# Last tile's columns in two pieces, the first FFN columns closed one by one, and another order for the first attention

## Chip, cores, metric

One core of a Trainium2 chip. The metric is the device time of one execution in microseconds (us), the median over several runs; lower is better. The profiler's span, from the first to the last recorded work of the core, is about 1.8 us shorter than the device time of the same run. Runs classed fast: for one core, executions up to 1.5% above the fastest.

## The reference, cut

```python
# q, k, v: (8 batches, 12 heads, 448, 64)
scores = q @ k.T / sqrt(64)
x = (maximum(scores, 0) ** 2 / 448) @ v          # -> (8, 448, 768)
xn = (x - mean) / sqrt(var + 1e-6) * g_ln
out = x + maximum(xn @ w_ch1, 0) @ w_ch2         # 768 -> 3072 -> 768
```

## The kernel before

The kernel carries its own list scheduler. Each piece of work is recorded with an estimated cost; TensorE's pieces are emitted in the program's order, and whatever the other engines can do by then is given to ScalarE or VectorE by estimated finish. What is built is fixed: each engine runs its list in order and waits on semaphores.

The attention of batch 0 has three groups of four heads (n = 0, 1, 2). For each, q and k are turned on TensorE ("T"), seven score blocks are made ("QK"), relu and square follow on ScalarE and VectorE, then seven products with v ("AV"). How the pieces interleave on TensorE is one string; `q` takes the next score piece, `a` the next of the others.

```python
FIRST_ORDER = "qaqqqqaqqqaaqqaaaaaqqaqqaqqaqaqqaaaaqqaaaqaaaaaaa"
...
av_stream = [("T", 0, 1)]        # turning of the far piece of k, columns 3 to 6 of group 0
for n in range(NPER):
    if n < NPER - 1:
        av_stream.append(("T", n + 1))
    av_stream += av_of(n)
    qk_stream += qks(n, 0, J)
...
for c in FIRST_ORDER:
    p = (av_stream if c == "a" else qk_stream).pop(0)
    PIECE[p[0]](*p[1:])
```

The rows of group 0 are loaded on SyncE's queue in three pieces (all of q; k columns 0 to 2; the "far" k columns 3 to 6); everything else is loaded on GpSimd's queue, at most eight transfers at a time. The score blocks 0 to 2 need the near piece of k only.

```python
for i, (t, j0, j1) in enumerate(((0, 0, J), FIRST[2], FIRST[3])):
    ...
    ld[t, j0] = R.add("SP", 480.0, emit, [], key=float(i), load=(2 * P, (46.0, 40.0, 90.0)[i]))
```

The first three columns of the first FFN product share 18 matmuls, and all three evictions wait for the last of them:

```python
for i, ki in enumerate(k_order(b)):
    def emit(eng, i=i, ki=ki):
        for ni in range(3):
            nc.tensor.matmul(st[ni][0], w1[:, ki, ni * P:(ni + 1) * P], xc[b][:, ki, :], ...)
    op = R.pe(570.0, emit, [ops["xc", b][i]] + ...)
for ni in range(3):
    h_evac(b, ni, st[ni], op, f_use if ni < 2 else slot_use)
```

The second FFN product makes each tile of 128 rows in two halves of 384 columns: 24 accumulating matmuls, one VectorE instruction that scales and adds x, then stores. The last tile (u = 3, m = 6) stores each half by itself.

Of the kernel before, what the change touches and what calls it, by code (L numbers as in the profile page):

```python
# [199 lines left out]
def kernel(  # L200
# [10 lines left out]
    nc = tc.nc  # L211
    P = 128
# [3 lines left out]
    Alu = mybir.AluOpType  # L216

    B, H, S, D = q.shape
    d_model = moe_g_ln.shape[0]
# [3 lines left out]
    K1 = d_model // P  # L223
# [4 lines left out]
    hd = d_model // 2  # L228
# [2 lines left out]
    POOL_BIAS = 1000.0  # L231
    N_FILL = 8

    FIRST_ORDER = "qaqqqqaqqqaaqqaaaaaqqaqqaqqaqaqqaaaaqqaaaqaaaaaaa"
    N_O = 2
    SUMMED = [0] + [2] + [NPER] * (B - 2)
    SQUARE_ON = (("DVE", "POOL"), (620.0, 1850.0))
# [19 lines left out]
    w1 = w_pool.tile([P, K1, d_ff], bf16)  # L257
    w2 = w_pool.tile([P, K2, d_model], bf16)
# [13 lines left out]
    def left(b):  # L272
        return slice(0, T) if b == 0 else slice(S - T, S)
# [12 lines left out]
    R = Order()  # L286
    stage, vt, qkT, xc, xm, mvs, rstd = {}, {}, {}, {}, {}, {}, {}
    ops = {}
# [8 lines left out]
    def big(tag, dims, **sizes):  # L297
        names = " ".join(sizes)
        n = 1
        for x in sizes.values():  # L300
            n *= x
        t = big_pool.tile([P, BIG], bf16, tag=tag)
        return t[:, :n].rearrange(f"p ({names}) -> p {names}", **sizes)
# [36 lines left out]
    def load_first():  # L340

        f = big_pool.tile([P, BIG // 2], fp32, tag=TURNED[1])
        raw = f[:, :4 * S].rearrange("p (t r c) -> p t r c", t=2, r=2)
        stage[0] = big(STAGE[0], None, t=2, r=H // 2, c=S)
        ld = {}
        for i, (t, j0, j1) in enumerate(((0, 0, J), FIRST[2], FIRST[3])):
            def emit(eng, t=t, cols=slice(j0 * D, j1 * D)):
                rows = (q, k)[t][0].rearrange("h (p j) d -> (h p) (j d)", j=J).rearrange("(pr r) c -> r pr c", r=P)
                nc.sync.dma_start(raw[:, t, :, cols], rows[:, 0::NPER, cols])  # L349
            ld[t, j0] = ld[t, j0 + 4] = R.add("SP", 480.0, emit, [], key=float(i), load=(2 * P, (46.0, 40.0, 90.0)[i]))  # L350
        ops["qk_ld", 0, 0] = []
        for t, j0, j1 in FIRST:
            cols = slice(j0 * D, j1 * D)

            def cast(eng, t=t, cols=cols):
                copy(eng, stage[0][:, t, 0::NPER, cols], raw[:, t, :, cols])
            ops["qk_ld", 0, 0].append(
                R.add(("DVE", "ACT"), (100.0 + 67.0 * (j1 - j0), 200.0 + 107.0 * (j1 - j0)), cast, [ld[t, j0]], key=-3.0))

    def copy(eng, o, i):  # L360
        if eng == "ACT":
            nc.scalar.copy(o, i)  # L362
        else:
            nc.vector.tensor_copy(o, i)  # L364
# [93 lines left out]
    def rows_of(t):  # L458
        return slice(t * T, (t + 1) * T)
# [414 lines left out]
    def k_order(b):  # L874
        return [pn + NPER * h for pn in range(NPER) for h in range(2)] if b < 2 else range(K1)

    def ffn_1_first(b):

        st = [{}, {}, {}]

        def fill(eng):
            for ni in range(2):
                ps = ps_f.tile([P, S], fp32, tag="f")
                st[ni][0] = ps
            ps = ps_s.tile([P, 2, 512], fp32, tag="s")
            st[2][0] = ps[:, 0, :S]
            for i in range(N_FILL):
                nc.tensor.matmul(st[i % 2][0][:, :3 * P], ones, x0_T[:, 0, S + T:], start=True, stop=True)
        R.pe(N_FILL * 163.0, fill, list(f_banks) + [slots[0]])
        for i, ki in enumerate(k_order(b)):  # L890
            def emit(eng, i=i, ki=ki):
                for ni in range(3):
                    nc.tensor.matmul(st[ni][0], w1[:, ki, ni * P:(ni + 1) * P], xc[b][:, ki, :],  # L893
                                     start=(i == 0), stop=(i == K1 - 1))
            op = R.pe(570.0, emit, [ops["xc", b][i]] + ([ops["w1", ni] for ni in range(3)] if i == 0 else []))
        for ni in range(3):
            h_evac(b, ni, st[ni], op, f_use if ni < 2 else slot_use)

    def ffn_1(b, ni):
# [18 lines left out]
    def h_evac(b, ni, st, op, use=f_use):  # L918
        def relu(eng):
            if b == 1:  # L920
                outs = ((h1[:, ni, 0:T], left(b)), (hb[ni // (K2 // 2)][:, ni % (K2 // 2), :], reg(b)))
            else:
                outs = ((h1[:, ni, h_cols(b)], slice(0, S)),)
            for o, c in outs:
                if eng == "ACT":
                    nc.scalar.activation(o, st[0][:, c], Act.Relu)  # L926
                else:
                    nc.vector.tensor_scalar(o, st[0][:, c], 0.0, None, op0=Alu.max)
        ev = R.add(("ACT", "DVE"), (560.0, 620.0) if b != 1 else (750.0, 740.0), relu, [op], key=-3.0)
        use(ev)  # L930
        ops["h", b, ni] = ev
        if ni == K2 - 1:
            ops["f1_end", b] = op

    o_st = {}
    o_ring = [DONE] * N_O

    def f2_deps(u, m, j, part, parts):
        n = K2 // parts
        b = 2 * u + (0 if m < 3 else 1)  # L940
        d = [ops["w2", (part + 1) * n - 1], ops["h", b, (part + 1) * n - 1]]
        if part == 0:
            d.append(f_banks[0])
        return d

    def ffn_2(u, m, j, part, parts):
        def stat(ki):
            if u == 0:
                if m <= 3:
                    c = m + 1 if m < 3 else 0  # L950
                    return h1[:, ki, c * P:(c + 1) * P]
                return hb[ki // (K2 // 2)][:, ki % (K2 // 2), (m - 4) * P:(m - 3) * P]
            if m < 3:
                return h1[:, ki, T + m * P:T + (m + 1) * P]
            if m == 3:
                return h1[:, ki, 3 * P:4 * P]
            return h1[:, ki, (m - 4) * P:(m - 3) * P]

        b = 2 * u + (0 if m < 3 else 1)

        def emit(eng):
            if part == 0:
                o_ps = ps_f.tile([P, hd], fp32, tag="f")
                o_st["ps"] = o_ps
            n = K2 // parts
            for ki in range(part * n, (part + 1) * n):
                nc.tensor.matmul(o_st["ps"], stat(ki), w2[:, ki, j * hd:(j + 1) * hd],  # L967
                                 start=(ki == 0), stop=(ki == K2 - 1))
        op = R.pe(975.0 * 4 / parts, emit, f2_deps(u, m, j, part, parts))
        if (m in (2, 6) or (u, m) == (0, 3)) and j == 1 and part == parts - 1:  # L970
            ops["f2_end", b] = op
        if part < parts - 1:
            return
        ps = o_st["ps"]
        ri = m if m < 3 else m - 3

        def evac(eng):
            if j == 0:
                o_t = o_pool.tile([P, d_model], fp32, tag="o")
                o_st[u, m] = o_t  # L980
            nc.vector.scalar_tensor_tensor(  # L981
                o_st[u, m][:, j * hd:(j + 1) * hd], ps, rstd[b][:, ri:ri + 1],
                xm[u, m][:, j * hd:(j + 1) * hd], op0=Alu.mult, op1=Alu.add)
        ev = R.add("DVE", 620.0, evac, [op, ops["rstd", b], o_ring[-N_O]], key=-3.0)
        f_use(ev)
        if j == 1:
            if m in (2, 6) or (u, m) == (0, 3):
                ops["f2_out", b] = ev
            if m == 3:
                ops["m3_out", u] = ev  # L990
        final = (u, m) == (B // 2 - 1, 6)
        if j == 0 and not final:
            return
        cols = slice(j * hd, (j + 1) * hd) if final else slice(0, d_model)
        blocks = {0: ((0, 0), (0, 1)), 1: ((0, 2), (0, 3)), 2: ((0, 4), (0, 5)), 3: ((1, 6), (0, 6)),
                  4: ((1, 0), (1, 1)), 5: ((1, 2), (1, 3)), 6: ((1, 4), (1, 5))}[m]
        if u == 0 and m <= 3:
            blocks = {0: ((0, 1), (0, 2)), 1: ((0, 3), (0, 4)), 2: ((0, 5), (0, 6)), 3: ((1, 6), (0, 0))}[m]
        for r, (bb, jj) in enumerate(blocks):
            def store(eng, r=r, bb=bb, jj=jj):  # L1000
                dst = out[2 * u + bb].rearrange("(p j) d -> j p d", j=J)[jj, :, cols]
                (nc.scalar if eng == "ACT" else nc.sync).dma_start(dst, o_st[u, m][rows_of(r), cols])
            sto = R.add("SP" if final and r else "ACT", 550.0, store, [ev], key=-0.5, load=(T, 150.0))
        o_ring.append(sto)
# [162 lines left out]
    with tc.manual_schedule():  # L1167
# [31 lines left out]
        means = 0  # L1199
        for c in FIRST_ORDER:  # L1200
            p = (av_stream if c == "a" else qk_stream).pop(0)
# [20 lines left out]
        for b in range(2, B):  # L1222
            u = b // 2
# [41 lines left out]
```

## Time and profile before

| | before |
|---|---|
| three runs | 541.95, 542.58, 542.9 us, median 542.58 |
| with three more beside the changed kernel | median 542.27 |
| the profiled run | 543.12 us, span 541.3 us |
| TensorE busy | 528.2 us, 98% of the span |
| first FFN group begins, after which TensorE has no listed idle | 30.03 us |

The rows behind this table are shown in the prediction. In a row of the view in order of time, the first number is the start in us, the second the time to the end of the group, then engine, source line, operation, destination and source, shape and count; the bracket is the engine's idle time before it and what ended it.

### The profile page before, as it was taken

What the parts mean: (1) busy time and instruction counts of PE and PEld (TensorE: products, weight loads), DVE (VectorE), ACT (ScalarE), POOL (GpSimd) and SP (SyncE); (2) the same over time, 40 slices, a digit from 0 to 9 for tenths busy, and PEclk for the clock granted to TensorE, in tenths of its full rate; (3) what the DMA queues carried; (4) which work ended last, traced back from release to release, by engine and by line L of the source; (5) the groups of instructions that cost most, each with busy time, mean ns of one, the idle gap of its engine ahead of it and who ended that gap; (6) DMA issues with size and microseconds to landing.
All of it is one profiled execution on the core that took longest, in us unless ns stands there. A gap on an engine that the chain in (4) does not pass through costs nothing.

```text
span 541.3 us, 9868 instructions
## 1 busy us (share of the span) xinstructions
PE 528.2 (98%) x4200; PEld 285.7 (53%) x4200; DVE 281.9 (52%) x483; ACT 232.6 (43%) x381; POOL 112.5 (21%) x129
## 2 busy tenths in 40 slices
PE   4899999999999999999999999999999999999996
PEld 3444455555554455555555455555555555555564
DVE  5988647438674556835366446752456525530011
ACT  5977612115425652556124653265422654044200
POOL 6411600221260124311061121600220102100000
PEclk9999999999999999999999999999999999999999
DMA  9999999997299204970189602990023100510022
GB/s 194 194 187 192 200 183 170 149 147 133 60 155 142 62 1 91 195 117 1 31 106 188 94 1 47 165 192 1 1 58 76 29 1 1 99 49 1 1 58 59
DMA packets 141400, 51.83 MB, mean 96 GB/s; under 512 B 121254, under 2 KB 137132, under 8 KB 141356
## 3 DMA queue, kind: packets, MB, share of 16 engines
q0 software_dynamic: 81072, 25.50, 43.5%
q1 hardware_dynamic: 55804, 14.88, 18.6%
q10 hardware_dynamic: 4480, 10.82, 7.2%
q8 instruction: 33, 0.54, 0.4%
q14 instruction: 11, 0.09, 0.0%
HBM read 51.91 MB, written 11.01 MB: 116 GB/s over the span
## 4 chain that ended last, share of the span: by engine, by line
PE 95%; DVE 3%; DMA 1%; issue 0%; SPq 0%; ACT 0%; DVEq 0%
PE o_ps L967 41%; PE ps L910 40%; PE sc L569 7%; PE ps L631 6%; DVE a L593 1%; DMA f<-in_k_dram 1%; PE ps L893 1%; DVE a L580 1%; PE ps L490 0%; DVE t L364 0%; PE ps L697 0%; PE slot L806 0%; SPq L349 0%; ACT a L834 0%; DVE a L845 0%
## 5 line engine op out<-in xcount | busy, mean ns | idle before, releaser
L910 PE MATMUL ps<-a,w 128*128 128x448 bf16 x1134 | 220.5, 353 | 0.0
L967 PE MATMUL o_ps<-w,h 128*128 128x384 bf16 x1200 | 199.9, 326 | 0.0
L910 PEld LDWEIGHTS <-w 128*128 128x128 bf16 x1134 | 108.3, 98 | 108.3 <-issue 10.6
L967 PEld LDWEIGHTS <-h 128*128 128x128 bf16 x1200 | 116.0, 98 | 81.6 <-issue 5.8
L926 ACT ACTIVATE h<-ps 128x448 bf16<-128x448 f32 (+1 forms) x168 | 89.2, 532 | 103.8 <-PE ps L910 102.0
L578 ACT ACTIVATE a<-sc 128x896 bf16<-128x896 f32 x102 | 90.3, 924 | 86.5 <-PE sc L569 84.2
L580 DVE TENSOR_SCALAR a<-sc 128x896 bf16<-128x896 f32 x57 | 62.0, 1087 | 108.9 <-PE sc L569 108.7
L593 DVE TENSOR_TENSOR a<-a 128x896 bf16<-128x896 bf16 x158 | 99.2, 669 | 2.4 <-ACT a L578 2.1
L981 DVE SCALAR_TENSOR_TENSOR o_t<-o_ps,r_t,x_all 128x384 f32<-128x384 f32 x56 | 34.4, 615 | 107.1 <-PE o_ps L967 106.8
L726 POOL TENSOR_TENSOR sum_t<-sum_t,xT_all 128x384 f32<-128x384 f32 (+2 forms) x25 | 19.4, 778 | 167.4 <-ACT xT_all L362 154.4
L569 PE MATMUL sc<-t 64*64 64x448 bf16 x672 | 48.6, 368 | 2.2 <-ACT a L578 1.2
L631 PE MATMUL ps<-a,v_t 64*64 64x448 bf16 x636 | 36.8, 353 | 0.7 <-DVE t L364 0.5
L724 POOL TENSOR_TENSOR sum_t<-xT_all 128x384 f32<-128x384 bf16 (+2 forms) x13 | 10.2, 791 | 124.7 <-DVE a L593 96.5
L834 ACT ACTIVATE a<-a,g_sb 128x448 bf16<-128x448 bf16 x38 | 22.2, 656 | 25.9 <-DVE a L827 24.8
L362 ACT CAST xT_all<-ps 128x768 bf16<-128x768 f32 (+3 forms) x39 | 22.2, 573 | 22.6 <-PE ps L631 14.6
L569 PEld LDWEIGHTS <-t 64*64 64x64 bf16 x672 | 17.5, 107 | 25.6 <-issue 18.5
L631 PEld LDWEIGHTS <-v_t 64*64 64x64 bf16 x672 | 20.0, 107 | 14.7 <-issue 3.9
L400 POOL DMA_DIRECT2D t<-in_q_dram x12 | 19.3, 1772 | 24.3 <-DMA t<-t 22.9
L967 PE MATMUL o_ps<-w,t 128*128 128x384 bf16 x144 | 23.7, 326 | 0.0
L400 POOL DMA_DIRECT2D t<-in_k_dram x12 | 23.7, 2526 | 0.0
L827 DVE TENSOR_TENSOR a<-xT_all,sum_t 128x768 bf16<-128x768 bf16 (+1 forms) x24 | 19.4, 852 | 6.7 <-ACT sum_t L819 6.5
L384 POOL DMA_DIRECT2D v_t<-in_v_dram x16 | 16.5, 1402 | 19.5 <-DMA w<-in_moe_w_ch_dram 11.1
(55 smaller groups left out, 183.4 us busy)
## 6 DMA issues: line engine op xcount, KB each, us to landing
out_dram<-o_t ACTq DMA_DIRECT2D x54, 192.0 KB, 2.8
v_t<-in_v_dram POOLq DMA_DIRECT2D x16, 336.0 KB, 15.0
w<-in_moe_w_ch_dram POOLq DMA_DIRECT2D x4, 1152.0 KB, 40.1
t<-in_q_dram POOLq DMA_DIRECT2D x12, 336.0 KB, 7.2
t<-in_k_dram POOLq DMA_DIRECT2D x12, 336.0 KB, 10.8
w<-in_moe_w_ch_dram POOLq DMA_DIRECT2D x4, 768.0 KB, 19.6
w<-in_moe_w_ch_dram POOLq DMA_DIRECT2D x1, 1536.0 KB, 29.5
t<-in_q_dram POOLq DMA_DIRECT2D x5, 224.0 KB, 10.1
```

What stands on the lines that cost most here:

```text
L362: nc.scalar.copy(o, i)
L400: nc.gpsimd.dma_start(stage[b][half * T:(half + 1) * T, t].rearrange("p j (h d) -> p j h d", d=D), src[b, half * 6:half * 6 + 6].rearrange ...
L569: nc.tensor.matmul(sc[rows_of(half), r, :S], qkT[b][rows_of(r), 1, s * NPER + pn, rows_of(half)], qT[:, :, pn, rows_of(half)], start=True, ...
L578: nc.scalar.activation(attn[n, s], st[0][:, :, :S], Act.Relu, scale=rc2)
L580: nc.vector.tensor_scalar(attn[n, s], st[0][:, :, :S], rc2, 0.0, op0=Alu.mult, op1=Alu.max)
L593: nc.vector.tensor_mul(attn[n, s], attn[n, s], attn[n, s])
L631: nc.tensor.matmul(av_st[n][half][rows_of(hh)], vt[b][rows_of(half), 2 * pn + hh, s * D:(s + 1) * D], attn[n, s][rows_of(half), hh, :], st ...
L834: nc.scalar.mul(o, o, g_sb[:, ki:ki + 1])
L910: nc.tensor.matmul(st[0], w1[:, ki, ni * P:(ni + 1) * P], xc[b][:, ki, :], start=(i == 0), stop=(i == K1 - 1))
L926: nc.scalar.activation(o, st[0][:, c], Act.Relu)
L967: nc.tensor.matmul(o_st["ps"], stat(ki), w2[:, ki, j * hd:(j + 1) * hd], start=(ki == 0), stop=(ki == K2 - 1))
L981: nc.vector.scalar_tensor_tensor(o_st[u, m][:, j * hd:(j + 1) * hd], ps, rstd[b][:, ri:ri + 1], xm[u, m][:, j * hd:(j + 1) * hd], op0=Alu. ...
```

## The change

Its intent: the last eviction and store get smaller (128 columns in place of 384); the first FFN columns can be evicted earlier; the first attention's order is made for a k piece that lands later than was assumed (the load's figure goes from 90 to 120, which is an estimate that the scheduler uses and no instruction).

```diff
--- before.py
+++ after.py
@@ -231,7 +231,7 @@
     POOL_BIAS = 1000.0
     N_FILL = 8
 
-    FIRST_ORDER = "qaqqqqaqqqaaqqaaaaaqqaqqaqqaqaqqaaaaqqaaaqaaaaaaa"
+    FIRST_ORDER = "qqaqaqqqqqqaaaqaqaaqaqaqqqaaaqaaqaaqqaaqqaaaaaaaa"
     N_O = 2
     SUMMED = [0] + [2] + [NPER] * (B - 2)
     SQUARE_ON = (("DVE", "POOL"), (620.0, 1850.0))
@@ -347,7 +347,7 @@
             def emit(eng, t=t, cols=slice(j0 * D, j1 * D)):
                 rows = (q, k)[t][0].rearrange("h (p j) d -> (h p) (j d)", j=J).rearrange("(pr r) c -> r pr c", r=P)
                 nc.sync.dma_start(raw[:, t, :, cols], rows[:, 0::NPER, cols])
-            ld[t, j0] = ld[t, j0 + 4] = R.add("SP", 480.0, emit, [], key=float(i), load=(2 * P, (46.0, 40.0, 90.0)[i]))
+            ld[t, j0] = ld[t, j0 + 4] = R.add("SP", 480.0, emit, [], key=float(i), load=(2 * P, (46.0, 40.0, 120.0)[i]))
         ops["qk_ld", 0, 0] = []
         for t, j0, j1 in FIRST:
             cols = slice(j0 * D, j1 * D)
@@ -887,13 +887,19 @@
             for i in range(N_FILL):
                 nc.tensor.matmul(st[i % 2][0][:, :3 * P], ones, x0_T[:, 0, S + T:], start=True, stop=True)
         R.pe(N_FILL * 163.0, fill, list(f_banks) + [slots[0]])
-        for i, ki in enumerate(k_order(b)):
-            def emit(eng, i=i, ki=ki):
-                for ni in range(3):
-                    nc.tensor.matmul(st[ni][0], w1[:, ki, ni * P:(ni + 1) * P], xc[b][:, ki, :],
-                                     start=(i == 0), stop=(i == K1 - 1))
-            op = R.pe(570.0, emit, [ops["xc", b][i]] + ([ops["w1", ni] for ni in range(3)] if i == 0 else []))
+        k = k_order(b)
+
+        def part(cols, i0, i1):
+            def emit(eng):
+                for i in range(i0, i1):
+                    for ni in cols:
+                        nc.tensor.matmul(st[ni][0], w1[:, k[i], ni * P:(ni + 1) * P], xc[b][:, k[i], :],
+                                         start=(i == 0), stop=(i == K1 - 1))
+            return R.pe(190.0 * len(cols) * (i1 - i0), emit, ops["xc", b][i0:i1] + [ops["w1", ni] for ni in cols])
+        for i in range(K1 - 2):
+            part(range(3), i, i + 1)
         for ni in range(3):
+            op = part([ni], K1 - 2, K1)
             h_evac(b, ni, st[ni], op, f_use if ni < 2 else slot_use)
 
     def ffn_1(b, ni):
@@ -943,7 +949,13 @@
             d.append(f_banks[0])
         return d
 
-    def ffn_2(u, m, j, part, parts):
+    def ffn_2(u, m, j, part, parts, c0=0, c1=hd):
+        final = (u, m) == (B // 2 - 1, 6)
+        if final and j == 1 and c1 - c0 == hd:
+            if part == 0:
+                ffn_2(u, m, j, 0, 1, 0, 2 * P)
+                ffn_2(u, m, j, 0, 1, 2 * P, hd)
+            return
         def stat(ki):
             if u == 0:
                 if m <= 3:
@@ -964,9 +976,9 @@
                 o_st["ps"] = o_ps
             n = K2 // parts
             for ki in range(part * n, (part + 1) * n):
-                nc.tensor.matmul(o_st["ps"], stat(ki), w2[:, ki, j * hd:(j + 1) * hd],
+                nc.tensor.matmul(o_st["ps"][:, :c1 - c0], stat(ki), w2[:, ki, j * hd + c0:j * hd + c1],
                                  start=(ki == 0), stop=(ki == K2 - 1))
-        op = R.pe(975.0 * 4 / parts, emit, f2_deps(u, m, j, part, parts))
+        op = R.pe(975.0 * 4 / parts * (c1 - c0) / hd, emit, f2_deps(u, m, j, part, parts))
         if (m in (2, 6) or (u, m) == (0, 3)) and j == 1 and part == parts - 1:
             ops["f2_end", b] = op
         if part < parts - 1:
@@ -979,19 +991,18 @@
                 o_t = o_pool.tile([P, d_model], fp32, tag="o")
                 o_st[u, m] = o_t
             nc.vector.scalar_tensor_tensor(
-                o_st[u, m][:, j * hd:(j + 1) * hd], ps, rstd[b][:, ri:ri + 1],
-                xm[u, m][:, j * hd:(j + 1) * hd], op0=Alu.mult, op1=Alu.add)
-        ev = R.add("DVE", 620.0, evac, [op, ops["rstd", b], o_ring[-N_O]], key=-3.0)
+                o_st[u, m][:, j * hd + c0:j * hd + c1], ps[:, :c1 - c0], rstd[b][:, ri:ri + 1],
+                xm[u, m][:, j * hd + c0:j * hd + c1], op0=Alu.mult, op1=Alu.add)
+        ev = R.add("DVE", 160.0 + 1.2 * (c1 - c0), evac, [op, ops["rstd", b], o_ring[-N_O]], key=-3.0)
         f_use(ev)
         if j == 1:
             if m in (2, 6) or (u, m) == (0, 3):
                 ops["f2_out", b] = ev
             if m == 3:
                 ops["m3_out", u] = ev
-        final = (u, m) == (B // 2 - 1, 6)
         if j == 0 and not final:
             return
-        cols = slice(j * hd, (j + 1) * hd) if final else slice(0, d_model)
+        cols = slice(j * hd + c0, j * hd + c1) if final else slice(0, d_model)
         blocks = {0: ((0, 0), (0, 1)), 1: ((0, 2), (0, 3)), 2: ((0, 4), (0, 5)), 3: ((1, 6), (0, 6)),
                   4: ((1, 0), (1, 1)), 5: ((1, 2), (1, 3)), 6: ((1, 4), (1, 5))}[m]
         if u == 0 and m <= 3:
```

## The prediction

> **What bounds the kernel now.** I read the page first, then the chain that ended last, then the first 30 us of each engine in order of time, then the last 20 us. The page's engine totals and slices (one digit is a fortieth, 13.5 us; tenths of the slice):
>
> ```profile
> span 541.3 us, 9868 instructions
> PE 528.2 (98%) x4200; PEld 285.7 (53%) x4200; DVE 281.9 (52%) x483; ACT 232.6 (43%) x381; POOL 112.5 (21%) x129
> ...
> PE   4899999999999999999999999999999999999996
> ...
> PEclk9999999999999999999999999999999999999999
> ```
>
> TensorE (PE) is full from the third slice to the last but one, at full clock. PE's own time order lists no idle after this row:
>
> ```profile
> 30.03 3.56 PE L893 MATMUL ps<-a,w 128*128 128x448 bf16 x18 [0.18 <-ACT a L834]
> ```
>
> So the time is three terms: the 30.03 us before PE becomes continuous, PE's work from there, and the tail after the last matmul. PE work can only be moved between places in the middle. The chain of waits at the end:
>
> ```profile
> 506.06 31.21 PE o_ps L967 x192
> 537.27 0.03 issue
> 537.30 0.62 DVE o_t L981
> ```
>
> Each 384-column matmul costs 31.21 us / 192 = 162.6 ns; the last eviction ends at 537.92, and 541.3 - 537.92 = 3.4 us go to issuing and landing the last store. The first 30 us are otherwise: PE waits many times, and VectorE (DVE) and ScalarE (ACT) run nearly without gaps from 9 us on. The rows that matter, in order of time:
>
> ```profile
> 6.78 0.59 PE L569 MATMUL sc<-t 64*64 64x448 bf16 x4 [0.73 <-DVE t L364]
> 7.42 0.92 ACT L578 ACTIVATE a<-sc 128x896 bf16<-128x896 f32 x1 [2.65 <-PE sc L569]
> 7.69 0.43 DVE L364 CAST t<-f 128x512 bf16<-128x512 f32 x1 [0.97 <-DMA f<-in_k_dram]
> 8.18 0.53 PE L490 MATMUL ps<-identity,t 64*64 64x64 bf16 x12 [0.81 <-DVE t L364]
> 8.52 0.83 POOL L424 DMA_DIRECT2D w<-in_moe_w_ch_dram  x1 [1.23 <-DMA t<-in_q_dram]
> 8.86 0.42 DVE L364 COPY t<-ps 128x512 bf16<-128x512 bf16 x1 [0.73 <-PE ps L490]
> ...
> 9.24 2.54 ACT L578 ACTIVATE a<-sc 128x896 bf16<-128x896 f32 x3 [0.91 <-PE sc L569]
> ...
> 10.17 0.70 POOL L332 DMA_DIRECT2D t<-in_q_dram  x1 [0.82 <-DMA t<-in_k_dram]
> ...
> 18.80 4.36 DVE L593 TENSOR_TENSOR a<-a 128x896 bf16<-128x896 bf16 x8
> ```
>
> What to see: the first scores come at 6.78. PE then stands 0.81 us for the far piece of k (landed about 7.67), whose turning comes next in its fixed order; ACT waits 0.91 us for the second scores. The two POOL rows date two loads: POOL's ninth load is held until the first is in (q of the second third of the heads, 8.52), the tenth until the second (k of it, 10.17).
>
> **What the Trainium skill says.** "TensorE: Matmul & The Clock Gate", section "Back-to-back issue gap": N/2.4 + 2.5 ns per matmul when warm, but for a stream of weight load plus matmul about 81 ns at N=128 and 131 at N=512. The trace has 162.6 ns at N=384, exactly the formula (160 + 2.5), and nothing like 131 at 512; N=128 with a full weight load occurs nowhere in it. The section "LDWEIGHTS (loading the stationary operand)" of that page gives P/1.2, or 107 ns for 128 columns; the trace has 98 ns. Whether that is the spacing at N=128 or only a latency the trace can't tell: 64-column loads show 107 to 124 ns each though 51 transposes, each with its own load, pass in 1.60 us. "DMA: Bandwidth & Descriptors", section "Latency and other measured facts", puts the fixed cost of a transfer at about 2 us; the trace agrees, the last 96 KB stores land 2.3 to 2.4 us after issue. So a smaller last store saves little.
>
> **The change, part by part.**
>
> (1) Last tile, second half. Before: 24 matmuls of 384 columns, one eviction, one pair of stores. After: 24 of 256, 24 of 128 with all 24 weight loads repeated (the built order has 24 matmuls and 24 loads more), two evictions, two pairs of stores. By the formula that the trace bears out, the 256 piece is 24 x 109.2 = 2.62 us. The 128 piece is 24 x 55.8 = 1.34 us if matmuls bind, 24 x 81 = 1.94 by the skill's stream figure, 24 x 98 = 2.35 if weight loads run one after another at their recorded length. I choose about 65 ns, nearer to the formula, since the formula was right at 384: 1.56 us. Sum 4.18 against 24 x 162.6 = 3.90: +0.28. The last eviction shrinks: evictions of the FFN's first product take 548 ns at 384 columns and 224 at 64, a slope of 1.01 ns per column; 615 - 256 x 1.01 = 356 ns, saving 0.26. The last store has rows of 512 B for 1,536 B; of the 2.3 us to landing I give it 0.15. The built waits show that the last eviction waits for PE alone, not for the stores of the piece before, and those were issued earlier: the 256 piece is evicted some 0.48 us after its 2.62 (0.486 for 256 columns), its issue (about 0.45) ends before the 128 piece is evicted. Tail: +0.28 - 0.26 - 0.15 = -0.13 us.
>
> (2) First three columns of the FFN closed one by one. The same 18 matmuls, no new instruction: four steps of three, then the last two steps column by column. Column 0 closes four matmuls (4 x 0.19 = 0.75 us) earlier and column 1 two. But PE went straight on with score matmuls at 33.59 and had no idle there, so nothing waits that could be given back. A cost may lie in the sixth centred piece being wanted at matmul 14 instead of 16: 30.03 + 13 x 0.19 = 32.5, and DVE's two gains end at 32.42. Just in time. Effect 0 to +0.05.
>
> (3) Order of the first attention. Same pieces, 27 of one kind and 22 of the other. After: two score blocks before the far k piece is turned (one before), then one more, then turning the second third at once, then six score blocks; before it did three score blocks first. Consequences, chased by hand with the durations above (first matmul of a score block to its relu 0.64 us, relu 0.83 in a row on ACT, 1.00 on DVE, squares 4.36/8, so 0.54):
> the second scores run at 7.15 and their relu follows the first at 8.25, not at 9.24: ACT gains 0.9. But DVE's order still puts the copy of the far piece (8.86, because k lands at 7.67) ahead of the first square, so DVE starts no earlier. The third relu ends near 10.0. Now PE stands at the k half of the second turning until 10.17, turns until about 11.0, and only then makes the fourth scores: relu at 11.6. ACT is idle 1.6 us where before it was idle 0.9. DVE's work from 8.86 to the last square: before 20 squares, 3 relus, 4 turned copies, 2 output copies = 10.8 + 3.0 + 2.0 + 1.1 = 16.9; after 20, 2, 5, 3 = 10.8 + 2.0 + 2.6 + 1.6 = 17.0. ACT gets a relu more (19 for 18) and loses a turned copy and an output copy. Chasing both on, the last square ends on DVE near 26.2 and on ACT near 26.4, against 26.3 and 26.1 before. Effect about +0.05 on the 30.03, with an error of my chase of some 0.5 either way. The larger load figure (120 for 90) is no instruction; it only shifts what the kernel's own scheduler believes.
>
> Further on the built order of PE shows only regroupings of FFN pieces with attention, of equal work: 0.
>
> Sum: -0.13 + 0.02 + 0.05 = -0.06; I lean a little towards gain, because a tuned order was presumably picked for one: 542.58 - 0.2 = 542.4 us.
>
> **Rivals.** (a) Weight loads bind at 128 columns: 2.35 us in place of 1.56, the tail grows by 0.66, about 543.2. For: 98 ns recorded. Against: the overlapping small loads. (b) PE's new early wait for the k load is longer or starves ACT and DVE both: start +0.5, 542.9 to 543.1. For: the load at 10.17 stands just ahead of six score blocks. Against: DVE has 17 us of work in any order and two squares and a copy to fill with. (c) The order pays: DVE loses its small holes, ACT finishes early since it has less to do, start -0.7, and the tail -0.35 at 56 ns: 541.5. For: ACT's sum shrinks by about 0.6. Against: DVE's does not. (d) The earlier closing frees banks and PE gains: nothing for it, as PE has no idle there.
>
> **Range and chances.** The three runs before spread 541.95 to 542.9, about 0.5 each way; start and tail add about 0.5 each. Range 541.4 to 543.3. Two per cent is 10.9 us, more than all idle in the start; nothing in reach does that: faster 0.01, same 0.98, slower 0.01.
>
> **What would show it.** In the changed profile: PE's continuous stretch begins at 29.5 to 30.5 (start); the L569 row after the second turning begins near 11.0 with ACT idle before its relu about 1.6 (my chase); the first FFN group shows no idle inside; the 24 last matmuls take 1.3 to 1.9 us; the last eviction 0.36 us, and 3.2 to 3.3 us from its end to the span's. I would be wrong if PE becomes continuous more than 1 us earlier or later, if the 128 piece takes over 2.2 us, or if a new idle appears in the middle.

## Result, and the profile after

| | before | after |
|---|---|---|
| median, six runs each | 542.27 us | 541.71 us |
| range | 541.95 to 542.9 | 541.68 to 542.41 |
| ratio of fast runs | | 0.9991, 95% interval 0.9978 to 1.0004 |
| span of the profiled run | 541.3 us | 539.9 us |
| first FFN group begins | 30.03 us | 28.93 us |
| last eviction begins | 537.30 us | 536.39 us |
| from there to the end of the span | 4.0 us | 3.5 us |

A ratio is the mean time of the one kernel's fast runs over that of the other's in the same rounds, so it isn't quite the ratio of the medians. The interval includes 1: this is "same" by the 2% rule, and even the 0.1% is not clear of noise as a plain comparison.

The page of the changed kernel, its span and engine totals (busy us, share, instructions):

```profile
span 539.9 us, 9924 instructions
PE 526.8 (98%) x4224; PEld 287.0 (53%) x4224; DVE 282.6 (52%) x487; ACT 231.3 (43%) x378; POOL 112.6 (21%) x129
```

There are 24 matmuls and weight loads more, as built. The changed kernel's VectorE in order of time at the end (the last two rows are the two pieces), and its chain of waits at the end (start, us, what):

```profile
532.43 0.62 DVE L993 SCALAR_TENSOR_TENSOR o_t<-o_ps,r_t,x_all 128x384 f32<-128x384 f32 x1 [3.28 <-PE o_ps L979]
...
535.05 0.48 DVE L993 SCALAR_TENSOR_TENSOR o_t<-o_ps,r_t,x_all 128x256 f32<-128x256 f32 x1 [2.00 <-PE o_ps L979]
...
536.39 0.35 DVE L993 SCALAR_TENSOR_TENSOR o_t<-o_ps,r_t,x_all 128x128 f32<-128x128 f32 x1 [0.85 <-PE o_ps L979]
```

```profile
505.10 31.27 PE o_ps L979 x216
...
536.39 0.35 DVE o_t L993
```

Evictions start as soon as their matmuls are done, so the distances between their starts are the matmul times: 535.05 - 532.43 = 2.62 us for 24 matmuls of 256 columns (109.2 ns each), and 536.39 - 535.05 = 1.34 us for 24 of 128 columns (55.8 ns each), against 3.90 us for the undivided half. Splitting costs 0.06 us of TensorE. The last eviction fell from 0.62 to 0.35 us, and from its end to the end of the span it is 539.9 - 536.74 = 3.16 us against 3.38.

The start of the changed kernel, in order of time, from TensorE, ScalarE, VectorE and GpSimd:

```profile
6.80 0.96 PE L569 MATMUL sc<-t 64*64 64x448 bf16 x8 [0.74 <-DVE t L364]
7.55 0.53 PE L490 MATMUL ps<-identity,t 64*64 64x64 bf16 x11
...
28.93 3.56 PE L896 MATMUL ps<-a,w 128*128 128x448 bf16 x18 [0.18 <-ACT a L834]
```

```profile
7.44 2.54 ACT L578 ACTIVATE a<-sc 128x896 bf16<-128x896 f32 x3 [2.62 <-PE sc L569]
10.22 8.30 ACT L578 ACTIVATE a<-sc 128x896 bf16<-128x896 f32 x10 [0.24 <-PE sc L569]
```

```profile
6.66 0.42 DVE L364 CAST t<-f 128x512 bf16<-128x512 f32 x1
8.22 0.42 DVE L364 COPY t<-ps 128x512 bf16<-128x512 bf16 x1 [1.15 <-PE ps L490]
```

```profile
7.23 0.88 POOL L424 DMA_DIRECT2D w<-in_moe_w_ch_dram  x1
8.05 0.76 POOL L332 DMA_DIRECT2D t<-in_q_dram  x1
```

The far piece of k is cast at 6.66 us, without a wait, where the profile of the kernel before has it at 7.69 after a wait for the load. The transfers' own view gives the landing of this piece (the last number is us from issue to landing), before and after:

```profile
f<-in_k_dram SPq DMA_DIRECT2D x1, 256.0 KB, 5.9
```

```profile
f<-in_k_dram SPq DMA_DIRECT2D x1, 256.0 KB, 3.9
```

The issue begins at 1.77 us in both, so the piece landed at about 7.7 and at about 5.7. The six further kernels below that load nothing more have 3.9 to 4.9 and the cast at 6.65 to 6.74: VectorE came to the cast only then, so in these profiles a landing up to about 6.7 us delays nothing. The two GpSimd rows had waited until 8.52 and 10.17 for earlier loads; here they don't wait at all. None of these loads depends on anything that was changed. So the two profiles differ by 1.10 us at the FFN group for two reasons mixed together, the order and when the loads landed, and the pair alone can't tell them apart.

### The profile page after: what moved, and what is told of

The parts are those of the page before. It is cut to its first block, busy times and chain, and to the rows that moved or that the text cites. A ratio compares the mean times of both kernels' runs of the same rounds, so it can differ in the third digit from the quotient of the medians.

```text
span 539.9 us, 9924 instructions
## 1 busy us (share of the span) xinstructions
PE 526.8 (98%) x4224; PEld 287.0 (53%) x4224; DVE 282.6 (52%) x487; ACT 231.3 (43%) x378; POOL 112.6 (21%) x129
## 4 chain that ended last, share of the span: by engine, by line
PE 95%; DVE 2%; ACT 1%; DMA 1%; issue 0%; ACTq 0%; DVEq 0%
PE o_ps L979 41%; PE ps L916 40%; PE sc L569 6%; PE ps L631 5%; DVE a L593 1%; PE ps L490 1%; DVE t L364 1%; PE ps L896 1%; DMA f<-in_q_dram 1%; ACT a L578 1%; PE ps L697 0%; PE slot L806 0%; DVE xT_all L364 0%; DVE a L580 0%; ACT a L834 0%
## 5 line engine op out<-in xcount | busy, mean ns | idle before, releaser
L979 PE MATMUL o_ps<-w,h 128*128 128x384 bf16 (+2 forms) x1224 | 200.1, 323 | 0.0
L979 PEld LDWEIGHTS <-h 128*128 128x128 bf16 x1224 | 117.4, 98 | 80.4 <-issue 5.7
L993 DVE SCALAR_TENSOR_TENSOR o_t<-o_ps,r_t,x_all 128x384 f32<-128x384 f32 (+2 forms) x57 | 34.7, 608 | 104.8 <-PE o_ps L979 104.6
L384 POOL DMA_DIRECT2D v_t<-in_v_dram x16 | 16.5, 1401 | 20.9 <-DMA w<-in_moe_w_ch_dram 18.0
## 6 DMA issues: line engine op xcount, KB each, us to landing
w<-in_moe_w_ch_dram POOLq DMA_DIRECT2D x1, 1536.0 KB, 29.2
```

The source lines that it names most:

```text
L979: nc.tensor.matmul(o_st["ps"][:, :c1 - c0], stat(ki), w2[:, ki, j * hd + c0:j * hd + c1], start=(ki == 0), stop=(ki == K2 - 1))
L993: nc.vector.scalar_tensor_tensor(o_st[u, m][:, j * hd + c0:j * hd + c1], ps[:, :c1 - c0], rstd[b][:, ri:ri + 1], xm[u, m][:, j * hd + c0:j ...
```

## Experiments

Two theories stood at this point. *Order*: the new order brings the FFN group from about 30 to about 28.9. *Loads*: the 1.1 us is mostly a difference in landing between two executions, which any kernel would show. Twelve kernels ran; the kernel before ran on the same chip. All gave correct results. All twelve are classed "same" at 2%, so what follows rests on profiles and on comparing groups of runs.

### The order alone

```diff
-    FIRST_ORDER = "qaqqqqaqqqaaqqaaaaaqqaqqaqqaqaqqaaaaqqaaaqaaaaaaa"
+    FIRST_ORDER = "qqaqaqqqqqqaaaqaqaaqaqaqqqaaaqaaqaaqqaaqqaaaaaaaa"
-  load=(2 * P, (46.0, 40.0, 90.0)[i])
+  load=(2 * P, (46.0, 40.0, 120.0)[i])
```

> The kernel before with only the new order of the first attention and the larger load figure. Theory 'order': continuous work on the first FFN matmul group begins about 28.9 us, where the changed kernel's profile has it, whatever the loads do, and the time falls by 0.3 to 1.1 us. Theory 'loads': the 1.1 us between the two profiles is mostly a difference in when the early loads landed in those two executions; then the time falls by under 0.2 us when runs with equally early loads are compared, the runs of both kernels spread over about 0.7 us in two groups, and in the profile the start of the FFN group follows the landing of the far k piece: near 28.9 with that cast at 6.7, near 30 with it at 7.7. The tail from the last matmul's end to the span's end stays as before, about 4.0 us.

Measured: 542.12 us median (542.08 to 542.20, and one run of 543.03), the kernel before beside it 542.07 (541.79 to 543.4); ratio 1.0 (0.9988 to 1.0013). The cast of the far piece was at 6.74 and the FFN group began at 28.98. From the last eviction's start to the span's end 4.05 us, as before. The order alone shows no gain: its four lower runs average 0.17 us more than the lower group of the kernel before, which the next experiment defines.

### The split tail alone

```diff
+        if final and j == 1 and c1 - c0 == hd:
+            if part == 0:
+                ffn_2(u, m, j, 0, 1, 0, 2 * P)
+                ffn_2(u, m, j, 0, 1, 2 * P, hd)
+            return
```

(with the column bounds of the change; old order, old closing.)

> The kernel before with only the last tile's second half in 256 and 128 columns. From the two profiles: the two pieces take 2.62 and 1.34 us where the one took 3.90 (+0.06), the tail from last matmul to end falls from 4.03 to 3.53 (-0.50). If these stand apart from the rest: time lower by 0.3 to 0.45 us than the kernel before, that is most of the whole change's 0.56 between medians. If the order is what pays: lower by no more than 0.2.

Measured: 541.86 us median of six: 541.29, 541.54, 541.83, 541.88, then 543.08 and 543.36. The first four average 541.63; of the 35 runs of the kernel before, the 21 below 542.4 (a cut made after the runs were seen) average 541.96. So 0.33 less, as expected, for runs of the lower group. In the profile (541.29 us) the last eviction begins 507.33 us after the FFN group (before 507.27, so +0.06), and the span ends 3.5 us later (before 4.0). And here is the old order with early loads, which no profile had shown yet (VectorE, then TensorE, in order of time):

```profile
6.66 0.42 DVE L364 CAST t<-f 128x512 bf16<-128x512 f32 x1
7.85 0.42 DVE L364 COPY t<-ps 128x512 bf16<-128x512 bf16 x1 [0.77 <-PE ps L490]
```

```profile
28.70 3.56 PE L893 MATMUL ps<-a,w 128*128 128x448 bf16 x18 [0.18 <-ACT a L834]
```

The old order begins the FFN group at 28.70, *earlier* than the new order's 28.93. So the 30.03 of the first profile was a run with late loads, and theory "order" has fallen.

### The closing alone

```diff
+        for i in range(K1 - 2):
+            part(range(3), i, i + 1)
         for ni in range(3):
+            op = part([ni], K1 - 2, K1)
             h_evac(b, ni, st[ni], op, f_use if ni < 2 else slot_use)
```

> The kernel before with only the first three FFN columns closed one by one. Both theories: no change (under 0.1 us), as TensorE has no idle after that group in either profile; the first of the three evictions starts 1.2 to 1.4 us after ScalarE's last gain in place of 1.6. A rival would be that earlier free banks let TensorE gain: 0.3 us or more.

Measured: 542.14 us median (lower group of four 542.01 to 542.22, two at 543.43 and 543.88); ratio 1.0005 (0.9992 to 1.0019). In the profile the 18 matmuls take 3.56 us as before, and the first eviction starts 1.22 us after ScalarE's last gain, where before it was 1.60. TensorE and ScalarE in order of time:

```profile
28.75 3.56 PE L896 MATMUL ps<-a,w 128*128 128x448 bf16 x18 [0.18 <-ACT a L834]
...
31.59 0.54 ACT L932 ACTIVATE h<-ps 128x448 bf16<-128x448 f32 x1 [1.22 <-PE ps L896]
```

TensorE doesn't notice: the first matmul of the second FFN product begins 67.20 us after the FFN group in both kernels. Later a difference appears: the matmul that sums for the fourth batch's mean begins 185.30 us after the group, before 185.16, and the same 0.13 us stays to the last eviction (507.40 against 507.27). In between the scheduler, whose estimates had moved, grouped second-product matmuls and attention pieces otherwise; the number of changes between tiled and full matmuls is the same in both. Why that grouping takes 0.13 us more was not settled. It goes with the grouping and not with the closing as such: the kernel of "One exchange in the order" below has the closing and the split tail, its matmul for the fourth batch's mean begins 185.16 us after the group, and its last eviction 507.32, which is 507.27 and the tail's 0.06.

### The changed kernel with the old order

```diff
-    FIRST_ORDER = "qqaqaqqqqqqaaaqaqaaqaqaqqqaaaqaaqaaqqaaqqaaaaaaaa"
+    FIRST_ORDER = "qaqqqqaqqqaaqqaaaaaqqaqqaqqaqaqqaaaaqqaaaqaaaaaaa"
```

(and 90 for 120.)

> The changed kernel with the old order and load figure put back. Theory 'loads' (order worth nothing): the same time as the changed kernel within 0.15 us in runs with equally early loads, 0.3 to 0.45 below the kernel before. Theory 'order': 0.3 us or more above the changed kernel, and the FFN group begins about 30 us.

Measured: 542.33 us median, in two groups: 541.5, 541.54, 541.73 and 542.93, 543.16, 543.25. The lower group is 0.12 us below the changed kernel's five (541.71). Its profile has early loads too. TensorE in order of time, the turning of the far piece and the FFN group:

```profile
7.16 0.52 PE L490 MATMUL ps<-identity,t 64*64 64x64 bf16 x11
...
28.69 3.56 PE L896 MATMUL ps<-a,w 128*128 128x448 bf16 x18 [0.18 <-ACT a L834]
```

(VectorE's copy of the turned piece begins at 7.84, against 7.85 in the profile of the tail alone.) This explains the 0.24 us. In the old order the far piece is turned at 7.16, right behind the first score block; in the new one a second score block runs first and the turning begins at 7.55. From the copy of the turned piece (7.84 old, 8.22 new), VectorE runs almost without gaps to the last square, so a later copy is a later everything. It also shows that what follows the copy is a little *shorter* in the new order: 28.93 - 8.22 = 20.71 against 28.69 - 7.84 = 20.85.

What the groups of runs showed gave a new theory, *insurance*: the new order pays 0.2 us while k is early, and gains when k is late, because the second score block then runs in time in which TensorE would stand anyway. The next six runs tested it.

### Loads made late on purpose, large dose, both orders

Based on the changed kernel with the old order and on the changed kernel; one load of no use goes on the same queue ahead of the far k piece, into a part of the buffer that nothing reads.

```diff
+                if i == 2:
+                    more = f[:, 4 * S:4 * S + 256].rearrange("p (r c) -> p r c", r=2)
+                    nc.sync.dma_start(more, rows[:, 1::NPER, :128])
                 nc.sync.dma_start(raw[:, t, :, cols], rows[:, 0::NPER, cols])
```

> The changed kernel with the old order, and one more load of 128 KB, of no use, on the same queue ahead of the far piece of k, so that this piece comes about 0.9 us later (the 256 KB piece itself took 1.75 us in the early profiles). Theory 'insurance': the new order costs 0.2 us when loads are early and saves when they are late; here the FFN group begins 29.8 to 30.3 us with the cast of the far piece at about 7.6, as in the one late profile so far (30.03), and the runs are 0.8 to 1.5 us above the early runs of the same kernel (541.5). Rival 'order is indifferent': both orders move by the same amount, and the group begins at most 29.3.

> The changed kernel with the same extra load. 'Insurance': the FFN group begins no later than 29.5 us, that is 0.4 or more ahead of the old order with the same delay, although with early loads it was 0.23 behind. 'Indifferent': it moves as the old order does and stays 0.2 behind it. Third theory, my blind chase: with late loads TensorE stands at the second turning, ScalarE starves, and the new order is 0 to 0.3 behind.

And with twice the columns in the extra load:

> The extra load doubled to 256 KB, old order: the far piece comes 1.75 us later than in early runs, its cast at about 8.4. 'Insurance': FFN group at 30.6 to 31.5.

> The extra load doubled, new order. 'Insurance': FFN group at least 0.5 us ahead of the old order with the doubled load, near 30.0. 'Indifferent': within 0.3 of it.

Measured (starts from the profiles; "after copy" is FFN start less copy start):

| run | cast of far k | copy starts | FFN group | after copy | times, us |
|---|---|---|---|---|---|
| 128 KB, old order | 10.45 | 11.60 | 32.67 | 21.07 | 543.35 to 546.09, median 544.3 |
| 128 KB, new order | 9.72 | 10.88 | 31.48 | 20.60 | 544.11 to 544.54, median 544.44 |
| 256 KB, old order | 9.98 | 11.14 | 32.04 | 20.90 | 544.69 to 545.56, median 545.07 |
| 256 KB, new order | 9.64 | 10.80 | 31.39 | 20.59 | 543.97 to 545.03, median 544.49 |

The dose was off: the piece's cast came 3.0 to 3.8 us later, not 0.9, and doubling the columns added nothing. The two orders also met different landings, and the medians of the first pair don't favour the new order. So the times alone decide nothing, but the last but one column does: once the copy starts, the new order needs 20.6 us, the old one 20.9 or more.

### The same with the smallest dose

```diff
+                if i == 2:
+                    nc.sync.dma_start(f[:64, 4 * S:4 * S + 128], rows[:64, 1, :128])
                 nc.sync.dma_start(raw[:, t, :, cols], rows[:, 0::NPER, cols])
```

> The old order with the split tail and a small extra load of 64 rows on the queue ahead of the far k piece, a quarter as many rows as the extra loads before that cost 3 us, so a delay of about 0.75. Theory 'two sides': in the old order the FFN group begins 20.85 to 21.2 us after the copy of the far k piece out of PSUM begins on VectorE; with that copy about 8.6 to 8.9 it begins at 29.5 to 30.0. 'Order indifferent' expects the same start in both orders.

> The new order, same delay. 'Two sides': the extra score block ahead of the turning costs 0.39 us only while k is early; once k is late by more than that the block runs in time that TensorE would stand anyway, and the FFN group begins 20.6 to 20.7 us after the copy: at equal copy times 0.2 to 0.5 us ahead of the old order. 'Indifferent': within 0.1. Chase of the prediction: 0 to 0.3 behind.

Measured: old order 544.26 us median (544.08 to 544.52), new order 543.93 (542.75 to 545.36). Even this load of 32 KB delayed the far piece's cast by 2.5 us. But by luck the two profiles met the same landing to 0.04 us, which is the clean pair. Old order, VectorE and then TensorE in order of time:

```profile
9.22 0.43 DVE L366 CAST t<-f 128x512 bf16<-128x512 f32 x1 [2.49 <-DMA f<-in_k_dram]
10.38 0.42 DVE L366 COPY t<-ps 128x512 bf16<-128x512 bf16 x1 [0.74 <-PE ps L492]
```

```profile
31.23 3.57 PE L898 MATMUL ps<-a,w 128*128 128x448 bf16 x18 [0.18 <-ACT a L836]
```

New order, the same two views:

```profile
9.18 0.43 DVE L366 CAST t<-f 128x512 bf16<-128x512 f32 x1 [2.45 <-DMA f<-in_k_dram]
10.34 0.42 DVE L366 COPY t<-ps 128x512 bf16<-128x512 bf16 x1 [0.73 <-PE ps L492]
```

```profile
30.94 3.56 PE L898 MATMUL ps<-a,w 128*128 128x448 bf16 x18 [0.18 <-ACT a L836]
```

Cast to copy is 1.16 us in both now (with early loads 1.19 old, 1.56 new): the price of the second score block has gone, since it ran while TensorE stood. The new order's FFN group is 0.29 us ahead, 0.25 of it after the copy. From copy to FFN group it is 20.85 us in the old order and 20.60 in the new, both as "two sides" had said. GpSimd's tenth load was held until 9.64 in the one profile and 9.13 in the other, that is until its second, k of the second group, had landed; TensorE has no listed wait for that k in either, so this doesn't disturb the pair.

"Insurance" holds in its sign: 0.24 behind with early loads, 0.29 ahead with late ones. Of its mechanism the lost price (0.37 us) is shown. Why the stretch after the copy is shorter in the new order, by 0.14 us with early loads and 0.25 with late ones, was not traced. And the late case is one pair of profiles: the medians differ the same way by 0.33 us, but the new order's six runs spread over 2.6 us.

How often it pays is less sure. Of all runs of the kernel before, 11 of 35 lay more than 0.7 us above the fastest, and so did 7 of 18 of the three experiments with the old order and no delay, each above its own fastest; with the new order (the changed kernel, the order alone, and the 64-column run below) it was 3 of 17. That points the expected way, but with such numbers it can be chance, and most of these runs have no profile that would show when their loads landed.

### One exchange in the order

An attempt at both advantages: turn the far piece first, as the old order does, and keep the rest of the new one.

```diff
-    FIRST_ORDER = "qqaqaqqqqqqaaaqaqaaqaqaqqqaaaqaaqaaqqaaqqaaaaaaaa"
+    FIRST_ORDER = "qaqqaqqqqqqaaaqaqaaqaqaqqqaaaqaaqaaqqaaqqaaaaaaaa"
```

> The changed kernel with only the second and third letters of the order exchanged, so that the turning of the far k piece comes ahead of the second score block as in the old order. 'Two sides': with early loads the copy of the far piece begins 0.38 earlier (7.84) and, if what follows stays 20.7 long, the FFN group begins at about 28.55, 0.38 ahead of the changed kernel and 0.15 ahead of the old order; time about 541.3. But the kernel's own scheduler hands out work on ScalarE and VectorE anew; if what follows is longer than 21.1, nothing is gained.

Measured: 543.53 us median (542.29 to 543.74), ratio to the kernel before 1.0016 (1.0002 to 1.003). It failed. The copy began at 7.84 as hoped, but the FFN group at 30.12, which is 22.28 us later. ScalarE in order of time:

```profile
7.43 2.54 ACT L578 ACTIVATE a<-sc 128x896 bf16<-128x896 f32 x3 [2.63 <-PE sc L569]
10.97 5.78 ACT L578 ACTIVATE a<-sc 128x896 bf16<-128x896 f32 x7 [1.01 <-PE sc L569]
```

ScalarE sat idle 1.01 us before the fourth relu, where the changed kernel has 0.24, and later VectorE waited 0.74 and 0.18 us for ScalarE. The scheduler had also divided the work anew: ScalarE got one output copy more, and its square came ahead of its last two relus. In this profile the k load of the second group came late (GpSimd's tenth load was held until 9.96), and TensorE stood for it in the middle of the second turning:

```profile
9.72 0.84 PE L490 MATMUL ps<-identity,t 64*64 64x64 bf16 x23 [0.43 <-DMA t<-in_k_dram]
```

Which share is the load's and which the division's stays open.

### A last piece of 64 columns

```diff
-                ffn_2(u, m, j, 0, 1, 0, 2 * P)
-                ffn_2(u, m, j, 0, 1, 2 * P, hd)
+                ffn_2(u, m, j, 0, 1, 0, 5 * P // 2)
+                ffn_2(u, m, j, 0, 1, 5 * P // 2, hd)
```

> The changed kernel with the last tile's second half cut at 320 and 64 columns. Theory 'columns bind': 24 x (320/2.4 + 2.5) = 3.26 us and 24 x (64/2.4 + 2.5) = 0.70, the last eviction about 0.29, the last rows 256 B: the evictions of the last two pieces begin 0.7 to 0.8 us apart, and the tail gains another 0.05 to 0.15. Theory 'weight load binds below 128 columns': the two evictions begin 1.0 us or more apart and the gain is lost.

Measured: 541.93 us median (541.9 to 542.01, one of 543.86), so 0.2 above the changed kernel's lower group. It was run at another time. VectorE's last two evictions:

```profile
535.75 0.55 DVE L993 SCALAR_TENSOR_TENSOR o_t<-o_ps,r_t,x_all 128x320 f32<-128x320 f32 x1 [2.64 <-PE o_ps L979]
536.45 0.28 DVE L993 SCALAR_TENSOR_TENSOR o_t<-o_ps,r_t,x_all 128x64 f32<-128x64 f32 x1
```

They begin 0.70 us apart: 29.2 ns per matmul with a full weight load each. Weight loads do not bind even here. The gain is lost further on. The rows of ScalarE's queue in this kernel and then in the changed kernel, both last stores together and the very last by itself (a DMA's row here is the time to issue it):

```profile
536.33 1.38 ACTq L1013 DMA_DIRECT2D out_dram<-o_t  x2
...
536.92 0.79 ACTq L1013 DMA_DIRECT2D out_dram<-o_t  x1
```

```profile
535.57 1.71 ACTq L1013 DMA_DIRECT2D out_dram<-o_t  x2
...
536.78 0.50 ACTq L1013 DMA_DIRECT2D out_dram<-o_t  x1
```

ScalarE's queue finishes issuing the two stores at 536.33 + 1.38 = 537.71, which is 0.98 us after the last eviction's end (536.73). In the changed kernel it is 535.57 + 1.71 = 537.28, 0.54 us after its end (536.74); the kernel before has 534.04 + 4.40 = 538.44, 0.52 us after. The last store's issue begins 0.19 us after the eviction's end in place of 0.04, behind the issue of the 320-column store, and takes 0.79 us in place of 0.50; why it takes longer is not shown. From the last eviction's start to the end of the span it is 3.65 us, against 3.51. With the piece before evicted 0.43 us ahead of the last eviction's end (536.30 and 536.73) the gain was lost, with 1.21 us (535.53 and 536.74) it was not; nothing between was tried. That the limit is about one issue time, 0.5 us, is an estimate from these two kernels.

No version beat both kernels clearly. With early loads the two kernels with the split tail and the old order are the lowest (lower groups at 541.63 and, with the closing, 541.59); with late ones the profiles favour the new order.

## Why the prediction was right or wrong

The time fell in the range (541.71 in 541.4 to 543.3), 0.7 below the forecast of 542.4, and the class was right. That is weaker than it looks: the unchanged 542.27 lies in the range too. And the sum of -0.06 came out by luck. With equally early loads the parts measure -0.46 (tail), +0.13 (middle) and +0.24 (start), together -0.09: three misses that cancel. The fastest runs agree: six of the 35 runs before lie at 541.79 to 541.81, five of the changed kernel's six at 541.68 to 541.79. So only about 0.1 of the 0.56 us between the medians is shown to be the change; the rest fits when the loads landed.

One of the prediction's own signs of being wrong came true: TensorE becomes continuous at 28.93, which is 1.10 us before 30.03, and more than 1 us was to mean wrong. It was no sign of the change, since the kernel before with early loads begins at 28.7. Step by step:

**What bounds the kernel** held. The middle is TensorE's and does not move: last eviction less FFN start is 507.27 us before and 507.46 after. But the first of the three terms was taken for a constant. The prediction read 30.03 from one profile; that run took 543.12 us, above all the timed ones, which could have been a warning. The old order with early loads has 28.7.

**Step 1, the tail**: right in sign, too small. Predicted +0.28 for the pieces, -0.26 for the eviction, -0.15 for the store, -0.13 in all. Measured +0.06, -0.27 and about -0.25 (from 3.38 to 3.43 us, in the three profiles with an undivided half, to 3.11 to 3.16, in the four with pieces of 256 and 128 and no added load), so -0.46 in all, and 0.33 in the times of the lower groups. Two terms were mis-sized. The 128-column spacing: 65 ns were chosen between the formula and the skill's stream figure, and the formula alone was right (55.8), which is 0.22 us. And the store, which gave 0.25 and not 0.15.

The 3.4 us were not all issuing and landing. By the DMA records of the packed trace, the last packet is in 2.06 us after the last eviction's end before and 1.72 us after; the other 1.37 and 1.43 us pass from there to the end of the span. All six kernels with an added load have 1.72 too, but 1.68 to 1.71 us from there to the end (3.38 to 3.47 together). Why that end is longer was not explained, but it is not the store. The rival that weight loads bind at 98 ns is refuted by the 64-column run.

**Step 2, the closing**: no effect on TensorE up to the second product, as said. The claim that the regroupings further on cost nothing failed by 0.13 us in this kernel.

**Step 3, the order**: the estimate of +0.05, with half a microsecond either way, contains the measured +0.24 (early) and -0.29 (late), but its reasoning failed in two places. It said that VectorE "starts no earlier", with k landing at 7.67; that fits the late pair (copies at 10.38 and 10.34), but in the changed kernel's profile k was early, and then VectorE starts 0.38 us later, since the second score block stands before the turning. And it said that TensorE would stand at the k half of the second turning and ScalarE be idle 1.6 us; in the changed kernel's profile that load was there and the idle time was 0.24. Both came from chasing one execution's landing times as if they were the kernel's. The exchange experiment shows TensorE standing there for 0.43 us and ScalarE idle for 1.01 us, in a run where that load did come late, so the wait is not imaginary, but it was not there in the profile that the prediction was about.

**Rivals**: (a) and (d) refuted, (b) not seen in the changed kernel, (c) right for the tail (56 ns) and wrong for the start: its 541.5 was nearer than the forecast, but not for its reason. That a tuned order was "presumably picked for a gain" was no argument from the profile; what the runs fit is an order picked for late loads.

## What to carry to other kernels

Before you credit a change with a difference in the start of a kernel, look at when its first loads landed in the two profiles, and compare the distance from the first work that waits for them, not from zero. An order of work that is best for early data can be worst for late data, so test it with the load delayed. When you split a last tile, count the issue time of the stores (0.5 us here): a piece evicted 0.43 us ahead of the last eviction's end was too close.

## What the Trainium skill lacked or had wrong

- "TensorE: Matmul & The Clock Gate", section "Back-to-back issue gap": it calls N/2.4 + 2.5 ns the gap of an isolated matmul and gives about 81 ns (N=128) and 131 ns (N=512) for a stream with a weight load per matmul. Here such a stream took 29.2 ns at N=64, 55.8 at 128, 109.2 at 256, 135.8 at 320 (3.26 us for 24) and 162.6 at 384, which is the formula each time.
- The same page, section "LDWEIGHTS (loading the stationary operand)": P/1.2 is 107 ns for 128 columns; the trace records 98 ns, yet a matmul with its own full load passes every 29.2 ns. The recorded loads overlap one another. The page does say elsewhere (section "Step-by-step: what each phase is for") that the next weights load while a matmul runs; that the length is no spacing it doesn't say in this section.
- "DMA: Bandwidth & Descriptors", section "Latency and other measured facts": it has a fixed cost of about 2 us per transfer, smaller with less load on HBM, and the last stores landed after 1.8 to 2.4 us. It does not say how much the landing of a kernel's first loads varies with nothing about them changed: the 256 KB far k piece landed 3.9 to 5.9 us after its issue here, its cast came at 6.65 to 7.69 us, and in the old order the FFN group began at 28.69 to 30.03.
- None of the pages that were read gives a figure for what an additional transfer ahead on the same queue costs while another queue is loading: with 32 KB in 64 rows the cast that waits for the next load came 2.5 us later, with 128 and 256 KB 3.0 to 3.8. Of the delay, 0.5 to 0.6 us is the issue of the additional transfer.
